# Attention, then two MLPs on one core: the second MLP's weight sums made later, and the planner's durations and priorities set anew

## The chip, the core and the metric

The kernel runs on one core of a Trainium2 chip. The metric is the device time of one execution in microseconds, as the median of several; here 968.92 us (three executions: 968.92, 970.71, 965.44). One more execution was taken with the hardware profiler; the rows below are from it. TensorE does the matmuls, VectorE (DVE) and ScalarE (ACT) the elementwise work, GpSimd (POOL) and SyncE (SP) here mostly issue transfers.

## What is computed

```python
x = attention(q, k, v)     # 4 batches, 8 heads, 576 positions of 64: sum of two softmax attentions,
                           # one global over positions pooled by 4, one over a band of 7 positions
x = x.transpose(0, 2, 1, 3).reshape(2304, 512)
h = x @ w_in               # first MLP, w_in 512 x 2048, w_out 2048 x 512
x = (h * cos(h)) @ w_out
h = x @ w_in2              # second MLP, the same sizes
y = (max(h, 0) ** 2) @ w_out2
```

The MLP weights come as 64-bit floats. The kernel turns each into a 32-bit float with integer operations, and splits every matmul operand into a rounded part and a rest (`hi`, `lo`), so that one product is three matmuls (`mm3`, L658 to L660).

## The kernel before

**Stages.** The attention is cut into 36 units: 4 global ones (`unit_g`) and 5 local ones (`unit_l`) for each batch. The first MLP goes over the 2304 tokens in five rounds of 512, 256, 512, 512 and 512 tokens, each in 16 slices `f` of 128 hidden columns: four groups of `mm3` for the hidden slice (`mlp_h`), then on ACT and VectorE `h * cos(h)` (L685, L689, L702, L694, L697) and the split (L264, L267), then four groups into four accumulators (`mlp_o`). Nine units come before the first round; 6, 9, 8 and 4 units are done beside rounds 0, 1, 2 and 3, those that the next round needs. In round 0 the weights are converted (`convert`) and the split `w_out` is stored; the later rounds load it back (`get_w2`, 512 KB a slice, three buffers). At the end of a round four accumulators are copied to `e` (L747, L749) and stored.

**The second MLP** has three rounds of 768 tokens in 8 pairs of slices; a pair's hidden part is made from seven products in place of eight (`big_h`, Strassen's scheme in Winograd's form). For that it needs sums of the weight blocks. `conv1` makes them for one pair: two loads of 512 KB (`rawi`, L771), their conversion (L775, L782, L787), four sums (L809), then four times a copy into a staging buffer on ACT (`rawo`, L822), the rest on VectorE (L825) and a store to memory (L830). `rawi` and `rawo` have two buffers each. `rawo` also takes the raw `w_out` of both MLPs.

**The order of the work.** The kernel isn't written in the order in which it runs. Every step is given to a planner, `op(engine, cost, key, fn, r, w, new)`: its engine, an estimated duration, a key, and what it reads, writes and allocates. `Plan.order` then simulates the five engines with these durations. At each point it takes the step that can begin first, and among those of one engine that can begin within 0.02 us the one with the lowest key. The order that comes out is the program of each engine; on the chip every engine runs its program in order and waits by semaphores. A transfer costs its issuer 0.5 us (SP) or 1.0 us (POOL), and all transfers share one queue in the simulation, each for its `cost`, plus 1.6 us (L177 to L180); 1.46 us stand for 512 KB. The key is a due time in the planner's own time. To it an offset is added from a table `OFF`, by the step's name and by one of five sections of the planner's time (0: before the first round, 1: round 0, 2: rounds 1 and 2, 3: rounds 3 and 4, 4: the second MLP). The table of before has entries for steps that no longer exist, and none for `conv1`, `get_w2b` and the steps named `big_`.

In the kernel before, `conv1`'s keys are spread from the start of round 2 to slice 10 of round 4, its loads 12 us earlier, and a load may be issued when all conversions of the first MLP's weights are done (the token `("conv",)`, L306 and L792).

While TensorE has nothing to do before the first `mlp_o`, the plan puts in small matmuls of zeros (L1164).

Of the kernel before, what the change touches and what calls it, by code (L numbers as in the profile page):

```python
# [50 lines left out]
OFF = {('PE|unit_g.f_s|ps|wps', 1): 42.1, ('ACT|softmax.f_norm|wp', 1): 8.0, ('PE|mlp_o.f_o|waccb', 1): 24.3, ('ACT|softmax.f_norm|wp', 0): 14.3, ('ACT|unit_l.f_x|wxr', 0): -12.7, ('PE|unit_g.f_t|ps|wps', 2): 36.4, ('PE|mlp_o.f_o|waccb', 2): 9.4, ('SP|convert.load|rawo|wrawo', 0): -134.5, ('DVE|convert.f2|wa|wwa', 1): 290.6, ('DVE|softmax.f_inv|wsm', 1): 577.5, ('DVE|mlp_h.f_r|t|wt', 1): -72.9, ('PE|mlp_h.f_h|ps|wps', 1): 6.7, ('PE|mlp_h.f_h|wps', 2): -260.5, ('PE|mlp_h.f_h|ps|wps', 2): -3.6, ('SP|body.<lambda>|wid', 0): -139.4, ('PE|unit_l.f_s|ps|wps', 1): 13.8, ('PE|unit_l.f_s|ps|wps', 2): 4.8, ('PE|unit_l.f_t|ps|wps', 2): 29.2, ('DVE|softmax.f_sub|wp', 2): -80.5, ('PE|unit_l.f_s|ps|wps', 3): -6.1, ('ACT|mlp_h.<lambda>|wt', 2): -96.8, ('DVE|convert.f1|wm|wwm', 1): 58.1, ('PE|mlp_h.f_h|ps|wps', 4): 6.4, ('PE|mlp_o.f_o|waccb', 4): 8.5, ('SP|convert.load|rawo|wrawo', 4): 115.0, ('SP|convert.load|rawi|wrawi', 0): -107.5, ('SP|get_w2.load|w2|ww2', 4): 101.0, ('ACT|split.f_hi|ww2', 1): -380.9, ('PE|unit_g.f_s|ps|wps', 2): 8.5, ('PE|unit_l.f_pv|ps|wps', 2): 27.1, ('PE|unit_l.f_t|ps|wps', 3): 34.9, ('ACT|split.f_hi|ww1h', 1): -222.3, ('DVE|split.f_lo|ww1l', 1): 187.5, ('PE|mlp_o.f_o|waccb', 3): 11.3, ('DVE|softmax.f_max|mx|wmx', 2): 135.4, ('DVE|convert.f1|wm|wwm', 0): 55.9, ('SP|load_pooled.ld|wk0', 0): -149.1, ('ACT|split.f_hi|gh|wgh', 2): -38.5, ('DVE|split.f_lo|ww2', 1): -87.0, ('PE|mlp_h.f_h|ps|wps', 3): -1.7, ('DVE|convert.f3|wwa', 1): 37.4, ('PE|mlp_h.f_h|wps', 3): -57.7, ('DVE|softmax.f_inv|wsm', 2): 46.0, ('ACT|unit_g.f_up|wup', 0): -123.8, ('SP|load_local.<lambda>|wkz', 0): 18.3, ('DVE|mlp_o.f_e|e|we', 2): -30.4, ('DVE|split.f_lo|wxl', 2): 35.3, ('DVE|softmax.f_sum|sm|wsm', 1): -35.6, ('DVE|split.f_lo|wxl', 1): -129.9, ('DVE|softmax.f_inv|wsm', 3): 210.4, ('SP|load_pooled.ld|wq0', 0): -60.3, ('DVE|mlp_h.f_g|wt', 4): -23.3, ('PE|unit_g.f_s|ps|wps', 0): -116.6, ('ACT|mlp_o.f_e|e|we', 2): -48.3, ('SP|mlp_o.f_s|wx2d', 4): 50.3, ('POOL|load_pooled.<lambda>|wqn', 0): -182.7, ('POOL|load_pooled.<lambda>|wkd', 0): -0.4, ('DVE|unit_g.f_q|wqd', 2): 78.7, ('ACT|unit_g.f_e|wpt', 2): 65.3, ('DVE|softmax.f_sub|wp', 3): 74.0, ('DVE|mlp_h.f_g|wt', 3): 8.6, ('POOL|body.<lambda>|wpz', 0): -19.9, ('ACT|mlp_h.f_k|ki|wki', 1): -17.0, ('DVE|unit_l.f_x|wxr', 0): -101.7, ('DVE|softmax.f_sum|sm|wsm', 2): 23.3, ('DVE|body.<lambda>|wqd', 0): 47.0, ('SP|convert.load|rawo|wrawo', 3): 109.7, ('PE|unit_g.f_t|ps|wps', 1): 9.0, ('DVE|convert.f2|wa|wwa', 4): -43.3, ('ACT|mlp_o.f_e|e|we', 3): 77.4, ('ACT|split.f_hi|gh|wgh', 4): 22.3, ('SP|mlp_o.f_s', 4): 37.7, ('DVE|split.f_lo|gl|wgl', 2): 58.0, ('ACT|unit_l.<lambda>|wpz', 2): -34.4, ('DVE|convert.f1|wm|wwm', 3): -61.7, ('DVE|mlp_h.f_r|t|wt', 3): -1.9, ('DVE|body.<lambda>|wid16', 0): 13.3, ('ACT|split.f_hi|wxh', 2): -34.7, ('DVE|softmax.f_norm|wp', 0): 36.0, ('DVE|softmax.f_max|mx|wmx', 1): 30.0, ('SP|mlp_o.f_s|wx2d', 2): 52.7, ('ACT|unit_g.f_e|wpt', 1): -21.0, ('SP|load_local.<lambda>|wkz', 1): 8.3, ('ACT|unit_g.f_e|wpt', 0): -8.3, ('DVE|body.<lambda>|wmask16', 0): -6.4, ('DVE|mlp_h.f_r|t|wt', 2): 0.7, ('DVE|split.f_lo|ww1l', 4): 42.4, ('DVE|convert.f2|wa|wwa', 3): -82.0, ('DVE|softmax.f_sub|wp', 0): -5.7, ('SP|convert.load|rawi|wrawi', 3): 47.0, ('SP|load_local.lq|q|wq', 1): -11.0, ('ACT|softmax.f_exp_sum|sm|wp', 1): -66.6, ('SP|get_w2.load|w2|ww2', 1): -2.0, ('SP|load_local.lq|q|wq', 0): -85.3, ('DVE|split.f_lo|ww1l', 0): -157.3, ('POOL|load_pooled.<lambda>|wqn', 1): 77.6, ('DVE|split.f_lo|ww1l', 3): 5.4, ('DVE|mlp_h.f_g|wt', 2): -13.4, ('DVE|softmax.f_max|mx|wmx', 3): -17.0, ('DVE|convert.f3|wwa', 0): -30.7, ('DVE|softmax.f_norm|wp', 2): -7.0, ('DVE|split.f_lo|wxl', 3): -10.0, ('ACT|softmax.f_exp|wp', 3): -41.6, ('ACT|mlp_h.f_r2|t|wt', 4): 13.0, ('SP|load_local.lq|q|wq', 2): 5.6, ('SP|get_w2.load|w2|ww2', 2): -6.0, ('ACT|split.f_hi|ww1h', 3): -17.3, ('DVE|split.f_lo|gl|wgl', 3): -41.7, ('POOL|load_pooled.<lambda>|wqn', 2): 27.3, ('ACT|softmax.f_exp|wp', 0): 11.3, ('SP|body.<lambda>|wmf', 0): -25.3, ('DVE|split.f_lo|ww2', 4): -65.4, ('ACT|mlp_h.f_sin|wt', 3): 5.0, ('DVE|softmax.f_sum|sm|wsm', 3): -22.3, ('ACT|mlp_h.f_k|ki|wki', 2): 23.0, ('ACT|split.f_hi|wxh', 4): 34.6, ('ACT|split.f_hi|gh|wgh', 3): 59.6, ('DVE|softmax.f_norm|wp', 1): -30.0, ('ACT|unit_l.<lambda>|wpz', 1): 59.0, ('PE|unit_g.f_pv|ps|wps', 0): -7.3, ('SP|convert.load|rawo|wrawo', 1): -107.6, ('DVE|load_pooled.add_q|wqd', 0): 25.6, ('POOL|load_pooled.<lambda>|wvd', 1): 13.3, ('PE|unit_g.f_t|ps|wps', 0): 31.7, ('SP|load_x2.<lambda>|wxr', 3): 28.3, ('ACT|softmax.f_exp|wp', 1): -19.3, ('POOL|load_pooled.<lambda>|wvd', 0): 24.0, ('DVE|mlp_o.f_e|e|we', 3): -4.0, ('SP|convert.load|rawi|wrawi', 1): -14.0, ('DVE|softmax.f_max|mx|wmx', 0): -43.0, ('POOL|load_pooled.<lambda>|wvd', 2): -9.7, ('DVE|load_pooled.add_k|wkd', 0): 62.0, ('DVE|mlp_h.f_g|wt', 1): 5.3, ('ACT|unit_l.<lambda>|wpz', 0): -11.0, ('PE|unit_l.f_pv|ps|wps', 3): 26.3, ('POOL|body.<lambda>|wkz', 0): 15.3, ('ACT|split.f_hi|ww1h', 4): -15.7, ('ACT|split.f_hi|ww1h', 0): 15.3, ('PE|unit_l.f_pv|ps|wps', 0): -18.0, ('DVE|unit_l.f_x|wxr', 3): 56.7, ('DVE|split.f_lo|wxl', 4): 28.0, ('SP|load_local.lv|v|wv', 1): 18.0, ('ACT|split.f_hi|wxh', 3): -2.0, ('PE|unit_l.f_t|ps|wps', 1): -45.7, ('ACT|mlp_h.f_k|ki|wki', 3): -5.0, ('DVE|split.f_lo|gl|wgl', 1): 7.3, ('ACT|mlp_h.<lambda>|wt', 1): -32.0, ('DVE|convert.f3|wwa', 3): 0.6, ('POOL|load_pooled.<lambda>|wgate', 0): 20.0, ('SP|get_w2.load|w2|ww2', 3): 4.0, ('ACT|split.f_hi|gh|wgh', 1): -15.7, ('PE|unit_g.f_pv|ps|wps', 1): -3.3, ('PE|unit_l.f_t|ps|wps', 0): -16.0, ('SP|load_local.lv|v|wv', 2): 1.0, ('DVE|softmax.f_sub|wp', 1): -8.0, ('DVE|convert.f2|wa|wwa', 0): 0.3, ('POOL|load_pooled.<lambda>|wgate', 2): -30.0, ('DVE|convert.f3|wwa', 4): 2.0, ('SP|get_w2.save|ww2d', 1): 10.3, ('DVE|body.setup|whalfpi', 0): 0.7, ('DVE|split.f_lo|gl|wgl', 4): -17.0, ('DVE|mlp_o.f_e|e|we', 4): 46.0, ('SP|load_local.lq|q|wq', 3): 1.7, ('PE|unit_l.f_s|ps|wps', 0): 19.0, ('ACT|unit_g.f_up|wup', 2): 16.0, ('SP|get_w2.save|ww2d', 4): -9.0, ('SP|get_w2.save|ww2d', 2): -2.0, ('SP|load_local.<lambda>|wkz', 2): -30.0, ('PE|mlp_h.f_h|wps', 4): -1.3, ('PE|unit_g.f_pv|ps|wps', 2): 16.0, ('ACT|softmax.f_exp_sum|sm|wp', 0): 2.0, ('ACT|mlp_h.f_sin|wt', 1): -11.0, ('DVE|softmax.f_inv|wsm', 0): -1.0, ('DVE|unit_g.f_q|wqd', 1): 30.0, ('ACT|unit_g.f_up|wup', 1): 4.0, ('DVE|softmax.f_sum|sm|wsm', 0): 30.0, ('DVE|softmax.f_norm|wp', 3): 30.0, ('SP|mlp_o.f_s|wx2d', 3): 30.0, ('POOL|load_pooled.<lambda>|wkd', 2): 1.0}
STG = (36, 140, 300, 440)


# [1253 lines left out]
```

## Time and profile before

| | |
|---|---|
| median of 3 executions | 968.92 us (965.44 to 970.71) |
| profiled execution | 968.87 us, span 967.1 us, mean granted clock 0.977 |
| TensorE busy | 912.2 us, 94% of the span |
| VectorE, ACT, GpSimd busy | 622.0, 449.4, 36.8 us |
| transfers | 204.07 MB, mean 211 GB/s |

Busy times are times in which the engine has an instruction at work; that of matmuls is modelled, and they overlap. The granted clock is a share of 2.4 GHz: 1.00 or, when the chip has throttled TensorE, 0.50 (1.2 GHz); a value between is a mean over a stretch. The DMA share is the mean busy share of the core's 16 DMA engines; it can come out a little over 1 in a short slice. Times of day ("at 186 us") count from the first instruction.

### The profile page before, as it was taken

To read this page: it belongs to the slowest core of one execution; us is meant where nothing else is said; L and a number is where in the kernel's file an instruction comes from. 1 tells how busy PE (TensorE), PEld (TensorE's weight loads), DVE (VectorE), ACT (ScalarE), POOL (GpSimd) and SP (SyncE) were. 2 spreads that over 40 slices of the span, in tenths; PEclk is the share of its full clock that TensorE was granted. 3 is DMA by queue.
4 is the path that set the end of the run, shared out by engine and by line. 5 is a ranking of instruction groups with operands and counts; after the bars stand their busy time and mean duration, and the time that the engine had idled before them with its cause. 6 is when DMAs were issued, how large, how long until landed. Compare 5 with 4: busy or idle time off the path is not lost.

```text
span 967.1 us, 14804 instructions
## 1 busy us (share of the span) xinstructions
PE 912.2 (94%) x5552; PEld 794.4 (82%) x5552; DVE 622.0 (64%) x1106; ACT 449.4 (46%) x889; POOL 36.8 (4%) x53
## 2 busy tenths in 40 slices
...
GB/s 293 275 267 168 236 177 197 288 301 278 257 322 293 236 250 152 116 102 95 108 176 173 94 219 286 295 271 245 247 253 192 183 184 186 215 209 178 186 153 87
DMA packets 82566, 204.07 MB, mean 211 GB/s; under 512 B 9280, under 2 KB 18240, under 8 KB 82496
## 3 DMA queue, kind: packets, MB, share of 16 engines
q1 hardware_dynamic: 77888, 191.33, 60.3%
...
q8 instruction: 44, 0.72, 0.3%
...
## 4 chain that ended last, share of the span: by engine, by line
PE 70%; DMA 16%; DVE 6%; ACT 5%; issue 1%; SPq 1%; POOL 0%; ACTq 0%; DVEq 0%; POOLq 0%
PE acc L658 9%; PE acc L659 9%; PE acc L660 9%; PE pp L660 6%; PE pp L659 6%; PE pp L658 6%; PE ps L658 5%; PE ps L659 4%; PE ps L660 4%; DMA rawi<-in_wi_dram 4%; DMA kd_sb<-in_kp_dram 2%; PE acx L1084 2%; PE acx L1086 2%; PE acx L1085 2%; DMA out_dram<-e 2%; DMA w<-w_dram 1%
## 5 line engine op out<-in xcount | busy, mean ns | idle before, releaser
L658 PE MATMUL acc<-gh,w 128*128 128x512 f32 (+1 forms) x320 | 121.9, 381 | 12.2 <-ACT e L749 6.2
L658 PE MATMUL ps<-xh,w 128*128 128x512 f32 (+1 forms) x320 | 125.4, 392 | 7.5 <-DVE t L697 7.5
L659 PE MATMUL ps<-xl,w 128*128 128x512 f32 (+1 forms) x320 | 120.3, 376 | 0.0
L660 PE MATMUL ps<-xh,w 128*128 128x512 f32 (+1 forms) x320 | 120.0, 375 | 0.0
L659 PE MATMUL acc<-gl,w 128*128 128x512 f32 (+1 forms) x320 | 119.0, 372 | 0.9 <-DVE gl L267 0.9
L660 PE MATMUL acc<-gh,w 128*128 128x512 f32 (+1 forms) x320 | 118.8, 371 | 0.0
L697 DVE TENSOR_TENSOR t<-t,ps 128x512 f32<-128x512 f32 (+1 forms) x80 | 50.5, 632 | 63.0 <-ACT t L694 62.6
L1016 DVE TENSOR_TENSOR c<-ua,pp 128x384 f32<-128x384 f32 x96 | 53.0, 552 | 54.9 <-PE pp L660 54.6
L1054 ACT ACTIVATE xh<-c 128x768 fp32r<-128x768 f32 x32 | 27.0, 843 | 130.0 <-DVE c L1046 129.9
L658 PEld LDWEIGHTS acc<-gh,w 128*128 128x128 f32 x320 | 61.2, 191 | 24.8 <-ACT e L749 6.6
L658 PEld LDWEIGHTS ps<-xh,w 128*128 128x128 f32 x320 | 62.4, 195 | 20.4 <-DVE t L697 8.3
L1016 DVE TENSOR_TENSOR ua<-ua,pp 128x384 f32<-128x384 f32 x72 | 39.7, 551 | 58.8 <-PE pp L660 58.8
L689 DVE SCALAR_TENSOR_TENSOR t<-ki,ps 128x512 f32<-128x512 int32 (+1 forms) x80 | 50.0, 629 | 33.2 <-ACT ki L685 32.6
L660 PEld LDWEIGHTS ps<-xh,w 128*128 128x128 f32 x320 | 62.3, 195 | 10.5
L659 PEld LDWEIGHTS acc<-gl,w 128*128 128x128 f32 x320 | 61.3, 192 | 11.0 <-DVE gl L267 1.3
L660 PEld LDWEIGHTS acc<-gh,w 128*128 128x128 f32 x320 | 61.2, 191 | 10.7 <-DVE w L267 0.4
L659 PEld LDWEIGHTS ps<-xl,w 128*128 128x128 f32 x320 | 62.6, 196 | 8.9
L685 ACT ACTIVATE ki<-ps 128x512 int32<-128x512 f32 (+1 forms) x80 | 43.0, 546 | 48.8 <-PE ps L660 48.1
L702 ACT ACTIVATE t<-t 128x512 f32<-128x512 f32 (+1 forms) x80 | 46.7, 586 | 34.3 <-DVE t L689 33.5
L267 DVE TENSOR_TENSOR gl<-t,gh 128x512 fp32r<-128x512 f32 (+1 forms) x80 | 50.5, 633 | 17.8 <-ACT gh L264 17.4
L264 ACT ACTIVATE gh<-t 128x512 fp32r<-128x512 f32 (+1 forms) x80 | 46.6, 584 | 30.4 <-DVE t L697 29.1
L694 ACT ACTIVATE t<-t,halfpi 128x512 f32<-128x512 f32 (+1 forms) x80 | 54.0, 678 | 1.8
(163 smaller groups left out, 2112.0 us busy)
## 6 DMA issues: line engine op xcount, KB each, us to landing
w<-w_dram SPq DMA_DIRECT2D x96, 512.0 KB, 3.9
gh<-w_dram SPq DMA_DIRECT2D x84, 256.0 KB, 3.0
gl<-w_dram SPq DMA_DIRECT2D x84, 256.0 KB, 3.0
rawo<-in_wo_dram SPq DMA_DIRECT2D x32, 512.0 KB, 4.8
rawi<-in_wi_dram SPq DMA_DIRECT2D x32, 512.0 KB, 7.7
w_dram<-w SPq DMA_DIRECT2D x32, 512.0 KB, 3.8
w_dram<-rawo SPq DMA_DIRECT2D x24, 512.0 KB, 5.7
v<-in_vw_dram SPq DMA_DIRECT2D x20, 256.0 KB, 5.8
```

Of the source, the lines that this page charges most:

```text
L264: nc.scalar.activation(out=hi(), in_=src(), func=AF.Copy)
L267: nc.vector.tensor_tensor(out=lo(), in0=src(), in1=hi().bitcast(F32), op=OP.subtract)
L658: nc.tensor.matmul(ps, w_hi, r_hi, start=first, stop=False)
L659: nc.tensor.matmul(ps, w_hi, r_lo, start=False, stop=False)
L660: nc.tensor.matmul(ps, w_lo, r_hi, start=False, stop=last)
L685: nc.scalar.activation(out=tt(ki), in_=tt(hp), func=AF.Copy, scale=1.0 / TWO_PI)
L689: nc.vector.scalar_tensor_tensor(out=tt(t), in0=tt(ki), scalar=-TWO_PI, in1=tt(hp), op0=OP.mult, op1=OP.add)
L694: nc.scalar.activation(out=tt(t), in_=tt(t), func=AF.Sin, scale=-1.0, bias=halfpi[:, 0:1])
L697: nc.vector.tensor_tensor(out=tt(t), in0=tt(t), in1=tt(hp), op=OP.mult)
L702: "ACT", act(n), key + 0.2, lambda: nc.scalar.activation(out=tt(t), in_=tt(t), func=AF.Abs), w=[t]
L1016: nc.vector.tensor_tensor(out=out(), in0=a(), in1=ps(), op=OP.subtract if sub else OP.add)
L1054: nc.scalar.activation(out=gpart(0, R, f), in_=T[t], func=AF.Copy)
```

## The change

Three things are changed. `conv1` for the eight pairs is no longer emitted in round 2 (`n == 2`), but one pair at every fourth slice of rounds 3 and 4. Its key is the slice's due time plus 6 us, its loads' 6 us less, and a load waits for the last group of `mm3` of that slice (the token `("at", r, f)`) and not for the conversions. In the planner, the cost of a transfer is multiplied by 1.24 (SP) or 1.4 (POOL). The table `OFF` is replaced as a whole; the new one has entries for all steps of the present kernel. One setup step on VectorE gets a key that puts it first.

```diff
+OFF = {('SP|body.<lambda>|wid', 0): 5.5,
...
+('POOL|load_pooled.<lambda>|wvd', 0): -249.1,
+('SP|load_local.lq|q|wq', 0): 13.0, ('SP|load_local.<lambda>|wkz', 0): 229.3, ('SP|load_local.lv|v|wv', 0): -462.5,
+('SP|convert.load|rawi|wrawi', 0): -11.5,
...
+('ACT|split.f_hi|gh|wgh', 1): -1118.0,
+('PE|mlp_o.f_o|waccb', 2): 980.7,
+('SP|conv1.load|rawi|wrawi', 3): 427.3, ('ACT|conv1.f_hi|rawo|wrawo', 3): -97.3,
+('SP|get_w2b.load|rawo|wrawo', 4): 264.8,
+('SP|big_h.f_w|gh|wgh', 3): -108.5, ('SP|big_h.f_w|gl|wgl', 3): -232.9,
...
 class Plan:
+    RATE = {"SP": 1.24, "POOL": 1.4}
...
-                dma = max(dma, free[e]) + cost
+                dma = max(dma, free[e]) + cost * self.RATE[e]
...
         op("DVE", dve(512), key + 0.02, f3, r=[raw], w=[a])
-        plan.writer.setdefault(("conv",), []).append(len(plan.ops) - 1)
...
+        plan.writer[("at", r, f)] = [len(plan.ops) - 1]
         key += 0.5
...
-    def conv1(key, step, p):
+    def conv1(key, step, p, after):
...
-            op("SP", 1.46, k - 12.0, load, r=[("conv",)], w=[raw], new=[raw])
+            op("SP", 1.46, k - 6.0, load, r=[after], w=[raw], new=[raw])
...
-    op("DVE", 0.1, -1.0, setup, w=[("halfpi",)])
+    op("DVE", 0.1, -2000.0, setup, w=[("halfpi",)])
...
-        if n == 2:
-            step_c = (when[0, ORDER[4], 10] - t_r) / PAIRS
-            for p in range(PAIRS):
-                conv1(t_r + step_c * p, step_c, p)
...
             mlp_h(0, r, f, t_f)
+            at = NF * (n - 3) + f
+            if at >= 0 and at % 4 == 0 and at // 4 < PAIRS:
+                conv1(t_f + 6.0, 4.0 * step[r], at // 4, ("at", r, f))
```

## Rows read from the trace of the kernel before

**Rows 1.** Busy time by stage: stretch, its length, then each engine's busy time.

```profile
0.00:66.10 66.10, 51.61 (x678) 46.21 (x678) 49.87 (x113) 36.48 (x141) 13.59 (x24) 0.92 0.97 279
66.10:160.00 93.90, 91.09 (x471) 72.10 (x470) 82.94 (x151) 72.33 (x140) 3.31 (x4) 0.98 0.62 196
160.00:192.00 32.00, 26.05 (x197) 21.88 (x191) 27.09 (x63) 19.23 (x40) 8.09 (x11) 0.95 0.94 272
192.00:240.00 48.00, 38.72 (x300) 36.78 (x300) 26.25 (x60) 29.99 (x76) 2.04 (x3) 0.89 0.87 288
240.00:290.00 50.00, 42.40 (x333) 36.11 (x332) 39.02 (x86) 35.31 (x76) 5.38 (x8) 0.90 0.90 290
290.00:365.00 75.00, 72.42 (x390) 57.51 (x389) 56.09 (x108) 55.64 (x112) 4.39 (x5) 1.00 0.82 261
365.00:577.00 212.00, 211.46 (x1061) 172.40 (x1060) 111.46 (x178) 122.93 (x195) 0.00 (x0) 1.00 0.40 132
577.00:705.00 128.00, 125.35 (x705) 117.10 (x704) 110.22 (x173) 37.93 (x54) 0.00 (x0) 0.99 0.80 269
```

The busy times are those of PE (matmul), PEld (weight load), DVE, ACT and POOL, each with its count of instructions; then the clock, the DMA share and GB/s.

**Rows 2.** TensorE's waits from 190 to 330 us: total, times, longest.

```profile
PE acc L658 <- ACT e L749: 6.2, 1, 6.2
PE acc L658 <- DMA w<-w_dram: 5.9, 3, 4.4
PE ps L658 <- DVE t L697: 5.4, 2, 3.4
```

**Rows 3.** Busy time by stage again, in slices of 4 us.

```profile
188.00:192.00 4.00, 0.00 (x0) 0.00 (x0) 2.67 (x8) 0.36 (x1) 1.45 (x2) 0.59 1.08 277
...
204.00:208.00 4.00, 1.15 (x5) 1.18 (x6) 2.95 (x7) 2.88 (x9) 0.00 (x0) 0.72 1.04 363
208.00:212.00 4.00, 4.00 (x21) 4.00 (x20) 1.41 (x5) 1.00 (x4) 0.00 (x0) 0.50 0.97 398
...
280.00:284.00 4.00, 4.00 (x17) 3.23 (x17) 1.89 (x5) 0.94 (x2) 2.12 (x3) 0.89 1.03 386
```

**Rows 4.** Busy time in 160 to 365: instructions on `rawi` (DVE, ACT), L825, L822.

```profile
160.00:365.00 205.00, 51.89 (x96) 9.86 (x16) 0.94 0.87 276
160.00:365.00 205.00, 19.73 (x32) 0.94 0.87 276
160.00:365.00 205.00, 18.12 (x32) 0.94 0.87 276
```

**Rows 5.** Transfers issued from 160 to 365 us: count, size, time to landing.

```profile
DMA packets 19649, 56.62 MB, mean 276 GB/s; under 512 B 2424, under 2 KB 3960, under 8 KB 19632
...
w_dram<-rawo SPq DMA_DIRECT2D x24, 512.0 KB, 5.7
rawi<-in_wi_dram SPq DMA_DIRECT2D x16, 512.0 KB, 8.6
...
w_dram<-rawo SPq DMA_DIRECT2D x8, 256.0 KB, 5.0
```

**Rows 6.** Waits of ACT and SP's queue in 160 to 365, and ACT's timeline.

```profile
ACT rawo L822 <- DMA w_dram<-rawo: 15.6, 4, 7.4
...
SPq L830 <- DVE rawo L825: 41.7, 17, 7.0
...
203.39 0.63 ACT L822 ACTIVATE rawo<-rawi 128x512 fp32r<-128x512 f32 x1 [7.35 <-DMA w_dram<-rawo]
```

**Rows 7.** The chain that ended last: start, duration, what.

```profile
193.79 12.93 DMA w<-w_dram
...
231.67 9.03 DMA rawi<-in_wi_dram
```

**Rows 8.** Waits from 365 to 577 us.

```profile
ACT ki L685 <- PE ps L660: 36.0, 23, 5.0
```

**Rows 9.** TensorE's timeline: start, duration, then the gap ahead in brackets.

```profile
58.80 1.67 PE L608 MATMUL ps<-pz,v 128*64 128x116 f32 x16 [4.80 <-DMA v<-in_vw_dram]
...
66.09 0.48 PE L658 MATMUL ps<-xh,w 128*128 128x512 f32 x1
```

2 lines of the change are left out of this document (1 added, 1 removed).

## The prediction, made before the result was known

> **What bounds the kernel now.** I read the table by stage first, because the share of TensorE over the whole span mixes stages with different limits. The reader is to see in [rows 1] that TensorE is busy nearly all the time from 365 us on (211.46 of 212 us to 577, 125.35 of 128 to 705), and that it is not in two places: 0 to 66 us (51.61 of 66.1 busy, much of it filler matmuls) and 160 to 365. In the second place the four rows leave 5.95 + 9.28 + 7.60 + 2.58 = 25.4 us without a matmul, and the granted clock is 0.95, 0.89 and 0.90 in three of them. There the DMA share is 0.82 to 0.94; from 365 to 577 it is 0.40.
>
> Then I read whom TensorE waited for [rows 2]: 6.2 us for an eviction of an accumulator on ACT (L749), 5.9 us in three waits for a weight load (`w<-w_dram`), 5.4 us in two for a VectorE product (`t` L697). The clock by slices [rows 3]: in ten of 28 four-microsecond slices from 184 to 296 it is below 1; the first has no matmul at all, and 208 to 212 is wholly busy at 0.50, which is the 1.2 GHz level.
>
> Last, what stands behind those gaps. The weight sums of the second MLP (`conv1`) sit exactly there: 16 loads, 32 copies, 32 stores [rows 4, 5]. ACT waited 15.6 us in four waits, the longest 7.35, until a store of a staging buffer (`rawo`) had landed, and SP's queue stood 41.7 us at the `conv1` stores [rows 6]. The chain of waits goes through a `conv1` load of 9.03 us that lands at 240.7, with VectorE's queue standing behind it, and a `w` load of 12.93 us [rows 7].
>
> **The change part by part.** All sums are made against the profiled execution: 968.87 us, of which the span is 967.1; the median shown, 968.92, is the same time for this purpose.
>
> *1. conv1 leaves 160 to 365.* It takes with it 51.89 us of VectorE on `rawi` and of the 19.73 of L825 the half that isn't in this, so 61.8 us at most, and 18.1 us of ACT [rows 4]; and 16 x 512 + 24 x 512 + 8 x 256 KB = 23.1 MB of 56.62 MB of transfers [rows 5]. VectorE falls there from 27.09 + 26.25 + 39.02 + 56.09 = 148.5 us to 86.7, the transfers from 276 GB/s to 33.5 MB / 205 us = 163. Which gaps go? ACT's eviction (6.2) waits for a store that is queued among `conv1` traffic; the loads of `w` (5.9) are late with the queues full; L697 (5.4) stands in VectorE's queue behind a `conv1` instruction that waits for its load. That is 17.5 of 25.4 us. What is late next is the softmax chain (score, maximum, exponent, transpose), which has most of the other 7.9 us; I take a fifth of these as gone, since it shares VectorE and ACT with `conv1`. Taken: -19. The ends are -25.4 (all gaps) and -9.3 (rival A).
>
> *2. The clock.* Half-level time in 160 to 290 is 2 x (0.05 x 32 + 0.11 x 48 + 0.10 x 50) = 23.8 us [rows 1]. Work done at half rate costs half of its time: 11.9 us if all of it was busy, 0.5 if all 22.8 us of the gaps there lay in it. The slices [rows 3] are of both kinds; adding up, over the ten, the lesser of half-level time and busy time I get 18.4 us, so about 9. It goes with the gaps: 9 x 19 / 25.4 = 7. Taken: -7.
>
> *3. conv1 arrives in the last two rounds.* One pair goes to every fourth slice, gated by that slice's last product. In 365 to 577 VectorE rises from 111.5 to 173.3 of 212 us (0.82), ACT from 122.9 to 141.0 (0.67), the transfers from 132 to 132 + 23.1 MB / 212 us = 241 GB/s [rows 1, 4, 5]. The cover is TensorE's lead: ACT waits there for TensorE, not the other way (36.0 us in 23 waits, the longest 5.0) [rows 8]. The nearest stage with such a load is 66 to 160: VectorE 0.88, ACT 0.77, TensorE still 91.09 of 93.9 [rows 1]. So the ends are 0 and its loss scaled, 2.81 x 212 / 93.9 = 6.3. The new wait is on SP: a `conv1` load stands in SP's queue until the slice's product is done, and behind it stand the `w2` loads, which wait for TensorE as well and have three buffers. Taken, halfway: +3. If the cover is gone, rival D.
>
> *4. Durations of the planner.* Loads now count 1.24 times 1.46 us per 512 KB, so 1.81 us, those of GpSimd 1.4 times. From 0 to 66 us the trace moved 279 GB/s at a DMA share of 0.97 [rows 1], which is 1.88 us per 512 KB; in 208 to 212 it was 398 GB/s [rows 3], 1.32 us. So the new figure fits the crowded stretches, which are the ones that stall, and is too long for plain `w` loads. An order made with it puts fewer instructions in front of data that isn't there. I give it no term of its own.
>
> The Trainium skill ("DMA: Bandwidth & Descriptors", Specifications) gives some 358 GB/s as the HBM limit of a core; that would be 1.46 us per 512 KB (an estimate from that page), the planner's old figure. By it the scaling would be wrong and the new order too cautious; the 279 GB/s of the first stage speak against it, the 398 GB/s of one slice for it.
>
> *5. New priorities, start.* The first product of the first MLP starts at 66.09 us, and shortly before, TensorE waits 4.80 us for a `v` load [rows 9]. The new offsets put `v` far ahead (-462.5) and `kz` behind (+229.3). Ends: -4.8 for that wait, +9.0 if one more transfer as long as that in [rows 7] comes onto the chain. Taken, towards the row of the wait: -3.
>
> *6. New priorities, elsewhere.* At the start of the second MLP TensorE idles 2.65 us (577 to 705 in [rows 1]). The weights it begins with are put forward (-108.5, -232.9), while the conversions of its output weights are put back and share `rawo` with the last pair of `conv1`. Ends -2.65 and as much above; taken -1. From 705 on TensorE does the same products as before: 0. The setup instruction moved to the front costs nothing, since VectorE has no data then.
>
> Sum: -19 - 7 + 3 - 3 - 1 = -27, so 968.9 - 27 = 942 us.
>
> **The rivals.**
>
> *A, round 1 stays bound by its own transfers.* It is the short round (256 columns), so a `w` load of 512 KB is wanted twice as often, and nine attention units load beside it. For it: at 192 to 240 us, 288 GB/s x 48 us = 13.8 MB are moved, of which `conv1`'s even share is 23.1 x 48 / 205 = 5.4; the rest, 8.4 MB, in some 36 us that the stage would last without gaps and half clock, is 234 GB/s. Against it: a slice of 398 GB/s shows room. Then the 6.2 and 5.9 us and half of the 7.9 stay; 9.3 go, with 3 of the clock: 968.9 - 9.3 - 3 + 3 - 3 - 1 = 956.
>
> *B, the new order takes more.* All gaps (25.4) and the upper end of the clock term (11.9), the `v` wait and half of the other idle time of the start (4.8 + (14.5 - 4.8) / 2 = 9.7), the 2.65, nothing added: 49.7, so 919. For it: the old table has no entries for `conv1`, `get_w2b` or any `big_` operation, so those stood at raw priorities; the new one has them all. Against it: a static order meets transfers whose landing depends on what is queued ahead: 9.03 and 12.93 us for 512 KB each [rows 7].
>
> *C, no change.* A's small gain, and the start goes wrong by one transfer because `kz` is late instead of `v`: 956 + 3 + 9 = 968.
>
> *D, slower.* ACT runs in order. Each pair stages four copies through two `rawo` buffers, so the third and fourth copy wait for a store; the ACT wait of 7.35 us to 203.39 [rows 6] stood before the longest of the `w` waits, 4.4 us, and a half-clock stretch (two slices with 2 x (0.28 + 0.50) x 4 = 6.2 us at half level and 1.15 + 4.00 us busy, so 2.6 lost [rows 3]). In the last two rounds ACT's own slack is 5.0 us at most. A pair that stalls like this costs 4.4 + 2.6 = 7 us; against the gain of 30 it decides from the fifth of eight pairs on; with six, 968.9 - 30 + 42 = 981. Against it: the traffic there is lighter, 241 GB/s against 272 to 290.
>
> That the change doesn't do what it says is not a case: the code moves the loop and gates it.
>
> **How the numbers follow.** Forecast 942 (930 to 950): 0.49. A, 956 (950 to 964): 0.17. B, 919 (912 to 930): 0.18. C, 968: 0.08. D, 981: 0.08. A measurement of this kernel can tell about 0.5% (4.8 us) from no change. Faster by more are forecast, A and B: 0.84; within it C, 0.08; slower D, 0.08. The range leaves out D and the lowest part of B: 917 to 970.
>
> **What would show it.** In the trace after: no `conv1` instruction before the fourth round; 160 to 365 at a DMA share under 0.8, a clock of 0.97 or more, and TensorE gaps under 10 us; the first MLP over some 25 us earlier; the last two rounds at full TensorE with VectorE above 0.75. ACT waits of over 5 us at L822 in those rounds, with gaps on TensorE behind them, would make me wrong towards D; a first round that starts after 70 us, towards C; `w` waits that stay in round 1, towards A.

## The result: 1.2% faster, less than half of what was forecast

| | before | after |
|---|---|---|
| median of 4 executions | 969.82 us (965.44 to 971.2) | 957.34 us (955.92 to 959.62) |
| ratio, 95% interval | | 0.9881 [0.9842, 0.992] |
| profiled execution | 968.87 us, span 967.1 | 959.62 us, span 957.7 |
| first product of the first MLP starts | 66.09 | 68.52 |
| first MLP (to the first product of the second) | 506.4 | 488.6 |
| second MLP (to the start of the last matmul) | 386.6 | 394.6 |
| after the start of the last matmul | 8.0 | 6.0 |

The lower four rows are read from TensorE's timeline in the profiled executions. The first MLP became 17.8 us shorter. Of this the start gave back 2.4 us and the second MLP 8.0 us, and the end after the last matmul is 2.0 us shorter: 9.4 us in all, the difference of the two spans. The medians differ by 12.5 us; the profiled execution of the kernel after is the longest of its four, so some 3 us of the gain are in no stage of this table.

The table by stage of the kernel after has the columns of [rows 1].

```profile
0.00:68.50 68.50, 59.05 (x876) 53.58 (x877) 50.65 (x114) 37.09 (x142) 13.83 (x23) 1.00 0.97 278
68.50:557.10 488.60, 473.93 (x2726) 386.18 (x2724) 340.52 (x638) 308.04 (x613) 22.92 (x30) 0.99 0.65 205
160.00:200.00 40.00, 37.42 (x363) 31.24 (x362) 28.96 (x71) 31.86 (x81) 8.02 (x12) 1.00 0.88 231
200.00:240.00 40.00, 35.29 (x302) 32.77 (x302) 18.10 (x44) 23.74 (x70) 1.70 (x2) 1.00 0.61 186
240.00:285.00 45.00, 40.16 (x293) 32.71 (x292) 27.34 (x55) 26.82 (x54) 9.74 (x13) 0.92 0.88 221
285.00:365.00 80.00, 79.92 (x450) 63.37 (x448) 36.81 (x63) 52.48 (x104) 0.00 (x0) 1.00 0.33 105
365.00:556.90 191.90, 191.44 (x925) 154.12 (x925) 147.98 (x264) 114.51 (x197) 0.00 (x0) 1.00 0.70 242
557.10:951.70 394.60, 387.19 (x2161) 352.33 (x2159) 234.16 (x355) 79.01 (x113) 0.00 (x0) 1.00 0.66 213
```

The same view of the kernel before, for stretches that [rows 1] doesn't have:

```profile
66.10:572.50 506.40, 477.64 (x2716) 392.45 (x2714) 340.78 (x642) 334.31 (x634) 23.21 (x30) 0.97 0.63 200
365.00:575.10 210.10, 209.56 (x1051) 170.55 (x1050) 111.12 (x178) 122.93 (x195) 0.00 (x0) 1.00 0.40 130
572.50:959.20 386.70, 382.76 (x2164) 355.73 (x2162) 230.38 (x353) 77.42 (x113) 0.00 (x0) 1.00 0.68 215
```

The reader is to take length less PE busy in each row. In the first MLP, time without a matmul fell from 506.40 - 477.64 = 28.8 us to 14.7, and busy time, in which work done at half the clock takes twice as long, from 477.6 to 473.9. From 160 to 365 it fell from 25.4 to 2.58 + 4.71 + 4.84 + 0.08 = 12.2 us. The last two rounds carry `conv1` with TensorE as full as before (0.46 us idle, 0.54 before), with VectorE at 147.98 / 191.9 = 0.77 and the transfers at 242 GB/s. In the second MLP idle time rose from 3.9 to 7.4 us and busy time from 382.8 to 387.2, with the clock at 1.00 in both.

TensorE's waits of the kernel after, in the first MLP (columns of [rows 2]):

```profile
PE ps L584 <- DVE t L698: 4.3, 1, 4.3
PE ps L658 <- DVE t L698: 3.0, 5, 1.4
...
PE acc L658 <- DMA w<-w_dram: 0.4, 1, 0.4
```

Lines stand one higher than before (L697 is L698). The 5.9 us of `w` are 0.4, and the waits for `t` are much as they were [rows 2]. The eviction's 6.2 us are gone from this list, but not the wait itself. The longest wait for `t` is an eviction's, one round later. The three lines are from the timelines of ACT, VectorE and TensorE (start, duration, the instruction, the wait ahead in brackets):

```profile
269.07 0.38 ACT L750 ACTIVATE e<-acc 128x256 f32<-128x256 f32 x1 [4.75 <-DMA x_dram<-e]
272.04 0.69 DVE L698 TENSOR_TENSOR t<-t,ps 128x512 f32<-128x512 f32 x1 [6.99 <-ACT t L695]
272.79 1.12 PE L584 MATMUL ps<-id_sb,p 128*128 128x128 f32 x4 [4.33 <-DVE t L698]
```

ACT's queue stands 4.75 us until a store of `e` has landed, VectorE waits for what ACT makes next, and TensorE for VectorE.

ACT's waits of the kernel after, 365 to 561.5 us:

```profile
ACT ki L686 <- PE ps L660: 35.0, 21, 3.6
...
ACT rawo L823 <- DMA w_dram<-rawo: 3.7, 2, 3.4
```

ACT waits 3.7 us in all for a store of a staging buffer, where [rows 6] had 15.6, and still waits for TensorE as in [rows 8]. Rival D didn't happen.

### The profile page after: what moved, and what is told of

The parts are those of the page before. It is cut to its first block, busy times and chain, and to the rows that moved or that the text cites. A ratio compares the mean times of both kernels' runs of the same rounds, so it can differ in the third digit from the quotient of the medians.

```text
span 957.7 us, 15230 instructions
## 1 busy us (share of the span) xinstructions
PE 920.5 (96%) x5758; PEld 792.1 (83%) x5758; DVE 625.3 (65%) x1106; ACT 425.3 (44%) x869; POOL 36.7 (4%) x53
## 4 chain that ended last, share of the span: by engine, by line
PE 61%; DMA 7%; DVE 5%; ACT 3%; issue 1%; SPq 0%; ACTq 0%; DVEq 0%
PE acc L658 8%; PE acc L659 8%; PE acc L660 8%; PE pp L658 5%; PE pp L660 5%; PE pp L659 5%; PE ps L658 4%; PE ps L660 4%; PE ps L659 4%; DMA w<-w_dram 3%; PE acx L1085 2%; PE acx L1086 2%; PE acx L1087 2%; DMA rawo<-in_wo_dram 2%; DMA x_dram<-e 1%; PE ps L571 1%
## 5 line engine op out<-in xcount | busy, mean ns | idle before, releaser
L658 PE MATMUL ps<-xh,w 128*128 128x512 f32 (+1 forms) x320 | 121.7, 380 | 4.6 <-DVE t L698 3.0
L659 PE MATMUL ps<-xl,w 128*128 128x512 f32 (+1 forms) x320 | 118.0, 369 | 0.2 <-DVE xl L268 0.2
L660 PE MATMUL ps<-xh,w 128*128 128x512 f32 (+1 forms) x320 | 117.8, 368 | 0.0
L698 DVE TENSOR_TENSOR t<-t,ps 128x512 f32<-128x512 f32 (+1 forms) x80 | 50.5, 632 | 47.5 <-ACT t L695 47.0
L658 PEld LDWEIGHTS ps<-xh,w 128*128 128x128 f32 x320 | 60.2, 188 | 21.4 <-DVE t L698 9.0
L658 PEld LDWEIGHTS acc<-gh,w 128*128 128x128 f32 x320 | 60.5, 189 | 12.5 <-issue 2.4
L660 PEld LDWEIGHTS ps<-xh,w 128*128 128x128 f32 x320 | 60.3, 188 | 10.2
L659 PEld LDWEIGHTS ps<-xl,w 128*128 128x128 f32 x320 | 60.3, 189 | 9.6 <-DVE xl L268 0.5
L268 DVE TENSOR_TENSOR gl<-t,gh 128x512 fp32r<-128x512 f32 (+1 forms) x80 | 50.7, 634 | 25.6 <-ACT gh L265 25.4
```

The source lines that it names most:

```text
L268: nc.vector.tensor_tensor(out=lo(), in0=src(), in1=hi().bitcast(F32), op=OP.subtract)
L658: nc.tensor.matmul(ps, w_hi, r_hi, start=first, stop=False)
L659: nc.tensor.matmul(ps, w_hi, r_lo, start=False, stop=False)
L660: nc.tensor.matmul(ps, w_lo, r_hi, start=False, stop=last)
L698: nc.vector.tensor_tensor(out=tt(t), in0=tt(t), in1=tt(hp), op=OP.mult)
```

## The experiments

All are built from the two kernels. "Old table" and "new table" are the `OFF` of before and of after; "the move" is `conv1` in rounds 3 and 4; "SP's factor" is the figure by which the planner multiplies SP's transfers. All but e17 also have the setup step's new key, whose share no run separates. The stages are read as above; ratios are against the kernel before in the same session.

| kernel | median us | ratio [95%] | start | first MLP | second MLP |
|---|---|---|---|---|---|
| e1_move | 972.56 | 1.0036 [1.0011, 1.006] | 65.7 | 510.0 | 385.7 |
| e3_move_rate | 960.29 | 0.9918 [0.9888, 0.9948] | 77.5 | 487.1 | 388.3 |
| e4b_offsets_rate | 968.55 | 1.0006 [0.9982, 1.003] | 67.5 | 496.6 | 395.5 |
| e5_old_late | 957.65 | 0.9905 [0.9877, 0.9933] | 67.5 | 486.7 | 393.5 |
| e2_rate | 985.86 | 1.0167 [1.014, 1.0195] | 74.9 | 513.6 | 387.5 |
| e9_move_off | 996.07 | 1.0271 [1.024, 1.0303] | 66.7 | 507.5 | 411.8 |
| e10_move_sp | 947.83 | 0.9792 [0.9763, 0.9821] | 67.4 | 484.1 | 386.1 |
| e11_move_pool_lat | 974.38 | 1.0064 [1.0039, 1.009] | 77.4 | 500.0 | 385.9 |
| e12_stay_sp | 959.69 | 0.9907 [0.9868, 0.9947] | 68.1 | 493.4 | 386.6 |
| e13_move_sp118 | 959.43 | 0.9905 [0.9875, 0.9936] | 71.2 | 490.3 | 385.8 |
| e14_move_sp130 | 958.68 | 0.9898 [0.9851, 0.9945] | 73.5 | 488.1 | 386.0 |
| e15_after_pool1 | 969.15 | 1.0001 [0.9976, 1.0025] | 71.0 | 495.0 | 395.7 |
| e17_before_late | 988.88 | 1.0177 [1.0144, 1.021] | 66.6 | 506.8 | 411.2 |
| e18_after_nolate | 954.13 | 0.9835 [0.9807, 0.9862] | 68.5 | 492.8 | 386.5 |

The theory to test was that the move gives the gain and the new table spends part of it; the rival, that the durations give it, since they shape the whole order. Sorted by these two, the first MLPs of the table above and of the two kernels are:

| first MLP, us | SP's transfers as before | with SP's factor |
|---|---|---|
| `conv1` in round 2 | before 506.4, e17 506.8 | e12 493.4, e4b 496.6, e2 513.6 |
| `conv1` in rounds 3 and 4 | e11 500.0, e9 507.5, e1 510.0 | e10 484.1, e5 486.7, e3 487.1, e14 488.1, after 488.6, e13 490.3, e18 492.8, e15 495.0 |

With both, all eight are 11 us or more under the kernel before, with either table. The move without the factor gives nothing in two of three, and the factor without the move gives anything from -13.0 to +7.2. So it is the two together that are shown to shorten the first MLP; a size for each alone is not.

**The move alone (e1).** The kernel after with the old table and the old durations.

```diff
-OFF = {... new ...}
+OFF = {... old ...}
-    RATE = {"SP": 1.24, "POOL": 1.4}
-                dma = max(dma, free[e]) + cost * self.RATE[e]
+                dma = max(dma, free[e]) + cost
```

> The weight sums moved to the last two rounds, with the old table of offsets and the old transfer durations. Theory (the move itself frees the stretch 160 to 365, the new table costs some 7 us in the start and in the second MLP): gaps and half clock in the first MLP fall by 15 to 20 us and nothing is lost elsewhere, 948 to 955 us. Rival (the new offsets do it, the move alone leaves round 1 bound by its own loads): 962 to 970 us. A second rival: under the old table the sums stall the last two rounds, above 972.

It gained nothing: the first MLP took 510.0 us, and the theory's 948 to 955 us failed. Its 972.56 us lie in the second rival's range, but not for its reason: from 365 us on TensorE idles 0.5 us in the first MLP. The rows come from its table by stage, its ACT timeline and its DVE timeline:

```profile
65.70:575.70 510.00, 478.05 (x2720) 393.25 (x2717) 340.76 (x641) 336.31 (x634) 22.97 (x29) 0.97 0.62 198
...
189.63 0.60 ACT L749 ACTIVATE e<-acc 128x512 f32<-128x512 f32 x1 [4.11 <-DMA x_dram<-e]
...
293.11 0.92 DVE L485 COPY qd_sb<-qn_sb 64x576 f32<-64x576 f32 x2 [11.48 <-DMA qn_sb<-in_qp_dram]
294.06 0.69 DVE L697 TENSOR_TENSOR t<-t,ps 128x512 f32<-128x512 f32 x1
```

Gaps are 510.0 - 478.05 = 32.0 us, with no `conv1` there at all. The eviction still waits: ACT stands 4.11 us for the store of `e`. The kernel before has the same instruction in its ACT timeline:

```profile
191.64 0.60 ACT L749 ACTIVATE e<-acc 128x512 f32<-128x512 f32 x1 [4.28 <-DMA x_dram<-e]
```

So that wait is there without `conv1` too. And another one has grown: VectorE's queue stands 11.48 us at a copy for the pooled attention (4.26 at the same copy in the kernel before), ahead of `t`, for which TensorE waits. The chain of e1 (start, duration, what) shows what the copy waits for:

```profile
266.11 7.32 DMA kd_sb<-in_kp_dram
...
273.72 5.76 DMA kd_sb<-in_kp_dram
...
279.77 5.54 DMA kd_sb<-in_kp_dram
...
287.04 6.04 DMA qn_sb<-in_qp_dram
```

Four loads by GpSimd one after the other, 24.7 us in all: the first fills its tile, the later ones add to theirs, and each is issued when the one before it into its tile has landed. The plan had them landing sooner (0.82 + 1.6 us for one alone, after its issue) and put the copy ahead of work whose data was there. TensorE's timeline of e1 has the price:

```profile
294.80 1.43 PE L607 MATMUL ps<-pz,v 128*64 128x116 f32 x12 [11.15 <-DVE t L697]
```

A stand in a queue costs only what waits behind it, though. In e10 below, the fastest kernel, the same copy stands 8.93 us, and TensorE is busy all the while (its DVE timeline, then its table by stage):

```profile
285.76 0.93 DVE L486 COPY qd_sb<-qn_sb 64x576 f32<-64x576 f32 x2 [8.93 <-DMA qn_sb<-in_qp_dram]
...
268.00:290.00 22.00, 22.00 (x109) 17.89 (x108) 10.60 (x17) 10.60 (x18) 5.24 (x6) 1.00 0.84 185
```

**Move and durations, old table (e3); durations and new table, no move (e4b); the old table's offsets in the second MLP (e5).** e3 is e1 with `RATE` as in the change. e4b keeps `conv1` in round 2, its ten new entries left out. e5 takes the entries of section 4 from the old table.

```diff
-('SP|get_w2b.load|rawo|wrawo', 4): 264.8, ...   (e5: section 4 as in the old table)
```

> The move and the new transfer durations, old table of offsets. Theory (the durations matter little): within 3 us of the move alone. Rival (the order was bad because the planner held transfers for too short): 5 us or more below the move alone.

> The new offsets and durations, but the weight sums left where they were (round 2 on, without offsets of their own). Theory (the move frees the stretch): gaps of over 20 us and a clock under 0.96 stay between 160 and 365, and the start and the second MLP cost their 7 us, so 968 to 978 us. Rival (the offsets do it): 955 to 962 us.

> The changed kernel, but with the old table's offsets for steps whose due time lies in the second MLP. Theory (the new order of the second MLP costs the 4 us that it is longer): 392 us from the start of the second MLP to the end, total 952 to 955 us. Rival (the second MLP is longer because of what the first one hands over, the late sums): it stays at 396 and the total at 957.

e3 came out as its rival said, 12 us below e1. Its first MLP (487.1) is as short as after's, with the old table, so the new table isn't what shortens it; but its start is 77.5. e4b gained nothing in total, as its theory said, though its gaps from 160 to 365 us were 19.0 us and the clock there 0.97, not over 20 and under 0.96. e5 is 957.65 like after: its second MLP, 393.5, is hardly shorter, against its theory. Seven entries of section 3 for the second MLP's steps remained in it; that these are why wasn't tested by themselves. It left open where the 8 us come from.

**Durations alone (e2); move and new table, old durations (e9); durations of SP alone (e10); later landings for GpSimd (e11).** e10 and e11 answer to e3's late start: is it the long GpSimd durations?

```diff
 e10, old table, with the move:
-    RATE = {"SP": 1.24, "POOL": 1.4}
+    RATE = {"SP": 1.24, "POOL": 1.0}
 e11, old table, with the move, no RATE:
-                end[i] = dma + 1.6
+                end[i] = dma + (1.6 if e == "SP" else 5.6)
```

> The new transfer durations alone: the weight sums where they were, the old table of offsets. Theory (the old order puts instructions that wait for transfers too early into queues that run in order, so durations nearer to the measured ones help by themselves): 958 to 964 us. Rival (durations help only where the weight sums are out of the way, since the transfers fill the stretch anyhow): 966 to 972 us.

> The move and the new offsets, without the new durations. Theory (the durations are what the gain needs): 964 us or more, with a gap of several us at the pooled loads as in the move alone. Rival (the new offsets do the same work as the durations, either of them is enough beside the move): 955 to 960 us.

> The move with SP's transfers at 1.24 and GpSimd's left at 1.0, old table. Theory (the gap of 11 us of the move alone stands at GpSimd's pooled loads, so their duration decides): the gap stays, 966 to 972 us. Rival (it is the crowded queue as a whole, SP's loads are nine tenths of it): 958 to 963 us.

> The move, old table, SP's durations as before; only GpSimd's loads are told to land 4 us later than the planner thought (some 6.4 us after their issue for one alone, against 7.5 measured). Theory: the VectorE copy that waits for the pooled query moves back in VectorE's order, the gap of 11 us goes, 958 to 964 us. Rival (a replaced gap opens elsewhere as in every new order): 968 us or more.

e10 is the best kernel: 947.83 us, 2.1% under before, with the old table, and below both of its ranges. e2 lies above both of its own. e9 came out as its theory said, e11 as its rival. Longer GpSimd times in the plan, in either form, come with a start some 10 us later with the old table (e2 74.9, e3 77.5, e11 77.4; e1 65.7, e10 67.4), but e13 and e14 below start at 71.2 and 73.5 without them, so a part of this may be the order drawn. With the new table it is 68.5. Without the durations (e9) this table costs 996.07 - 957.34 = 39 us: none in the start (66.7), 19 in the first MLP, 17 in the second. Why the plan starts later with long GpSimd times wasn't followed further.

**Is it the move at all? (e12), is 1.24 special? (e13, e14), does after want GpSimd's 1.4? (e15).** e12 is e10 with `conv1` left in round 2; e13 and e14 are e10 with one figure changed.

```diff
-    RATE = {"SP": 1.24, "POOL": 1.0}
+    RATE = {"SP": 1.18, "POOL": 1.0}   (e13; 1.30 in e14)
 e15, new table, with the move:
-    RATE = {"SP": 1.24, "POOL": 1.4}
+    RATE = {"SP": 1.24, "POOL": 1.0}
```

> SP's transfers at 1.24, GpSimd's at 1.0, the old table, and the weight sums where they were: the best mix so far without its move. Theory (move and durations work only together: a right duration lets the plan see that the stretch is full, the move empties it): the first MLP takes 500 us or more from its first product to its last, as in each kernel with one of the two alone, total 962 to 985 us. Rival (SP's durations alone do it): 945 to 955 us.

> The move, SP at 1.18, GpSimd at 1.0, old table. Theory (a duration nearer to the measured one is what helps, and 1.18 is nearly as near): 945 to 955 us. Rival (the plan is a draw: each new order falls anywhere): outside of this, up to 975 us.

> The move, SP at 1.30, GpSimd at 1.0, old table. Theory: 945 to 955 us. Rival (a draw): outside of this, up to 975 us. If both this one and the one at 1.18 fall outside, the kernel at 1.24 was a lucky order and the durations no cause that can be carried over.

> The changed kernel with GpSimd's transfers at 1.0 in place of 1.4. Theory (the new table costs some 10 us in the second MLP, wherever the durations stand, and the first MLP stays near 487 us): second MLP 393 us or more after the last product of the first, total 950 to 962 us. Rival (the table fits only the durations that it was made with): 965 us or more, as without both scalings.

The first MLPs of e12 and e10 by stage:

```profile
68.10:561.50 493.40, 475.75 (x2719) 387.19 (x2717) 342.67 (x640) 337.63 (x635) 23.43 (x30) 0.99 0.63 206
```

```profile
67.40:551.60 484.20, 472.34 (x2720) 386.75 (x2718) 340.74 (x640) 339.84 (x637) 23.00 (x30) 0.99 0.65 210
```

One factor on SP's transfers, with `conv1` where it was, takes the gaps from 28.8 to 17.7 us and the first MLP from 506.4 to 493.4, which lies between e12's theory and its rival. It is one order: with GpSimd's factor beside it and no move (e2) the first MLP is 513.6. The move on top gives 9.3 more here (484.1), 8.0 from e4b to after, which differ in `conv1`'s entries too, and 26.5 from e2 to e3. With 1.18 and 1.30 and the move the first MLP is 490.3 and 488.1, and the start is later (71.2 and 73.5), so that they are 11 us slower in all than e10. Both fell outside 945 to 955 us, which the expectation named beforehand as the sign of a lucky order at 1.24: as far as three orders can tell, about half of e10's gain over before is that. The other half, some 10 us, all three have. e15 lost 12 us against after by one figure of the durations, as its rival said, and its second MLP is 395.7, as its theory said.

**The second MLP (e17, e18).** Forty entries of the new table name steps of the second MLP that the old one lacked (`operands`, `parts`, `combine`, `add` and all named `get_w2b` or `big_`). e17 is the kernel before with these forty added and nothing else; e18 is the kernel after without them.

```diff
+('SP|big_h.f_w|gl|wgl', 3): -232.9, ('PE|big_h.f_p|ps|wpp', 4): -118.6,
+('DVE|big_g.f_g|wc', 4): 506.7, ('DVE|get_w2b.f3|wwa', 4): -494.1, ...
```

> The kernel before, with the 40 new offsets of the second MLP's own steps put into its table (its products, sums, operands, weight conversions and stores) and nothing else. Theory (these offsets order the second MLP worse): it takes 392 us or more from the last product of the first MLP to the last one, against 384, total 975 to 982 us. Rival (the second MLP is longer because the late weight sums hand over a full queue): 384 to 387 us, total 968 to 972.

> The changed kernel without these 40 offsets. Theory: the second MLP takes 385 to 388 us, the first one stays near 488, total 947 to 952 us. Rival (the handover): the second MLP stays at 392 or more, total 955 us or more.

Both ways, as the theory said: added, the second MLP went from 386.6 to 411.2 us; taken out, from 394.6 to 386.5. The totals, 988.88 and 954.13, lie above the theory's ranges. The profiled executions of both are the longest of their six, 4.2 and 3.2 us over their medians. In all, e18 is only 3.2 us faster than after, and the intervals of the two overlap: its first MLP is 4.2 us longer, and the stretch from the end of the last matmul about 2 (7.5 to 8.3 us in each kernel without all of these entries, 5.6 to 6.4 with them). What the entries cost also hangs on the durations: without SP's factor the second MLP takes 411.2 (e17) and 411.8 (e9), with it 394.6 to 395.7 (after, e4b, e15). Of e17, the table by stage and TensorE's waits there:

```profile
573.30:984.50 411.20, 393.26 (x2160) 351.83 (x2159) 234.44 (x353) 78.81 (x113) 0.00 (x0) 0.99 0.62 202
...
PE acx L1084 <- DMA w<-w_dram: 11.3, 19, 1.9
PE pp L658 <- DVE ua L1016: 3.0, 2, 2.3
```

Of the kernel after, the same waits:

```profile
PE acx L1085 <- DMA w<-w_dram: 2.3, 5, 0.7
PE pp L658 <- DVE c L1017: 2.0, 2, 1.2
```

The second products wait for their `w` load, 19 times in e17 and 5 in after; the kernel before has no such wait. The SP timelines show how the loads are issued. First before, then after:

```profile
764.04 0.32 SPq L986 DMA_DIRECT2D gh<-w_dram  x1
766.17 0.32 SPq L986 DMA_DIRECT2D gl<-w_dram  x1
768.28 0.32 SPq L986 DMA_DIRECT2D gh<-w_dram  x1
770.38 0.32 SPq L986 DMA_DIRECT2D gl<-w_dram  x1
770.75 0.42 SPq L952 DMA_DIRECT2D w<-w_dram  x1
```

```profile
761.78 0.32 SPq L987 DMA_DIRECT2D gh<-w_dram  x1
762.16 0.42 SPq L987 DMA_DIRECT2D gl<-w_dram  x1
762.63 2.92 SPq L953 DMA_DIRECT2D w<-w_dram  x2
766.97 0.32 SPq L987 DMA_DIRECT2D gh<-w_dram  x1
767.49 0.32 SPq L987 DMA_DIRECT2D gl<-w_dram  x1
771.38 0.32 SPq L987 DMA_DIRECT2D gh<-w_dram  x1
```

In this stretch, a pair of weight tiles is loaded every 4.2 us before, evenly. After, the loads go out in bursts, two `w` close together. The waits of SP's queue from 720 to 930 us, before and then after, say what for:

```profile
SPq L986 <- PE pp L660: 125.9, 82, 1.7
SPq L986 <- PE acx L1086: 13.9, 7, 2.1
SPq L952 <- PE acx L1086: 12.7, 12, 1.1
...
SPq L952 <- PE acc L660: 1.3, 1, 1.3
```

```profile
SPq L987 <- PE pp L660: 131.1, 54, 5.7
SPq L953 <- PE acc L660: 24.7, 22, 3.6
```

About the same total, in 54 waits for the weight tiles where there were 89: SP stands up to 5.7 us at a load whose buffer isn't free, 2.1 before, and up to 3.6 at a `w` load, 1.3 before. What stands behind goes out late.

Only 3.5 of the 8.0 us are gaps that the trace shows. The other 4.4 us are in PE's busy time at an unchanged clock of 1.00. They are stalls that the modelled ends of the matmuls cover, as the starts show: in after, 74 products are followed by the next one over 0.03 us later than is the median for their shape, 16.0 us in all; before, it is 19 and 6.4 us. Of these, 59 (6.1 us) and 16 (2.0 us) show no gap. For most of them no row names a releaser. The loss builds up all along: counted from the second MLP's first product, its 500th starts 1.3 us later than before, its 1000th 3.1, its 2000th 6.7.

## Why the prediction was right and wrong

The direction held, and the time lies in the range. The forecast of 942 was 15 us too low, and 17.6 under the profiled execution (959.62), on which the stages are read: 9.0 in step 6, 5.4 in step 5, 5.2 in steps 1 to 3, less the 2.0 us at the end that no step has. These are its steps:

- **Step 6, second MLP: -1, and "From 705 on TensorE does the same products as before: 0". This failed, by 9 us.** It took 8.0 us more (386.6 to 394.6). The same products in another order, with loads in another order, are not the same time; e17 and e18 show that the forty entries do it, by `w` waits and by short stalls inside the busy time. I read the table for the handover only and priced its other entries at nothing.
- **Step 5, start: -3, measured +2.4.** The first product is at 68.52. The wait that the step priced did shrink, from 4.80 to 1.16 us, but it moved to the last unit before the first MLP, whose product came at 63.23 before. The start still hangs on a `v` load that is issued late (the timelines of SP and TensorE):

```profile
55.87 0.33 SPq L406 DMA_DIRECT2D v<-in_vw_dram  x1
...
65.89 0.99 PE L608 MATMUL ps<-pz,v 128*64 128x116 f32 x16 [1.16 <-DMA v<-in_vw_dram]
```

- **Steps 1 to 3, the first MLP: -19 - 7 + 3 = -23, measured -17.8.** The gaps from 160 to 365 fell by 13.2 us, against 19. Of the clock term 7, the busy time shows 477.6 - 473.9 = 3.7. (The slices behind that term add up to 19.4 us, not 18.4, which would leave it at 7.) The +3 for `conv1` in the last two rounds was 0: TensorE's lead held.
- **Step 1's reason fell all the same.** I read that `conv1` stood at the gaps and took it for their cause. With `conv1` gone and only the setup step's key changed beside it (e1) the gaps are 32.0 us: the eviction's wait is for the store of `e`, in after as well, and a queue that stands at the pooled copy takes the place of the rest.
- **Step 4, durations: "I give it no term of its own". Wrong in kind.** The move without SP's factor gives nothing (e1, e9); with it, all eight kernels have a first MLP 11 to 22 us shorter than before. The step's reason, that an order made with longer durations "puts fewer instructions in front of data that isn't there", fits: from 66 to 365 us the waits of VectorE and ACT for transfers add up to 35.3 us before and 28.0 in e1, but 7.4 in e12 and 13.3 in e10. That this is the cause isn't shown: e11, without the factor, has 9.6 us of them and a first MLP of 500.0, and in e10 the pooled copy still stands 8.93. I had not priced it, because I took every gap for `conv1`'s. The Trainium skill ("DMA: Bandwidth & Descriptors", Specifications) gives some 358 GB/s for a core, by which the old duration of 1.46 us per 512 KB would be right (an estimate from that page). The first stage of the kernel before moved 279 GB/s and one slice 398, on either side of it; as a planning figure, 1.18, 1.24 and 1.30 times the old duration all did better beside the move (490.3, 484.1, 488.1 against 510.0).

The rivals: after's 957.34 is A's 956 only in size. A's sign was `w` waits that stay, and they are 0.4 us. The largest loss lies in the second MLP, which no rival named. C's sign, a start after 70 us, is seen in e3 and not in after. Of the signs named, no `conv1` in the first three rounds, a DMA share of 0.61 and a clock of 0.98 there, and full last rounds came true; gaps under 10 us (12.2) and a first MLP that is over some 25 us earlier (15.4, at 557.1) did not.

What stays open: how SP's factor shortens the first MLP, why longer GpSimd times in the plan start it later, and the releaser of the 4.4 us inside busy time. Single terms under some 10 us also depend on the order drawn: e13 and e14 differ from e10 by that with only a duration changed. e18's first MLP, 4.2 us longer than after's, is within that.
